# Attention into gated experts, one core: conversions of w_out, w3 and the first gate weights at fixed steps, quarters of w3 @ w_out grouped

## The chip, the cores and the metric

One core of a Trainium2 chip runs the whole program in one launch. The metric is the device time of one execution in microseconds, lower is better. Three executions of the kernel before took 2013.15 us in the median (2010.26 to 2014.29).

## The reference, cut

```python
def phi(x):                                   # feature map, 64 -> 256
    proj = np.einsum('bhsd,df->bhsf', x, w_phi)
    proj = proj - np.max(np.abs(proj), axis=-1, keepdims=True)
    return np.concatenate([np.exp(proj), np.exp(-proj)], axis=-1)
q_p, k_p = phi(q), phi(k)                     # batch 4, heads 8, seq 576
kv = einsum('bhsf,bhsd->bhfd', k_p, v);  z = k_p.sum(2)
num = einsum('bhsf,bhfd->bhsd', q_p, kv); den = einsum('bhsf,bhf->bhs', q_p, z)
x = num / (den + 1e-6)                        # as 2304 tokens x 512
x = ((x @ w1) * (x @ w2)) @ w3 @ w_out        # first layer; w1, w2, w3, w_out arrive as float64
# second layer: 8 experts, gates P from 8 Sinkhorn rounds over softmax logits
out = sum over e of P[:, e] * (relu(x @ w1e[e]) @ w2e[e])
```

## The kernel before, in words

The program has three stages: attention, the first layer (two products `ab`, their elementwise product, then `px` with the folded weight w3 @ w_out), and the experts. The change lies in the first.

**Attention** works on 8 quads of four heads. A quad takes six steps, `k`, `q`, `k`, `q`, `k`, `q`, so there are 48 steps and eight more that drain the pipeline (the loop is lines 432 to 455). In each step a list of stages (line 432) issues one part of several older steps. `st_P` projects the step's q or k on TensorE into `pp` (12 matmuls, two PSUM buffers in turn). One step later `st_M` takes the largest absolute value (L184) and subtracts it (L186) on VectorE. `st_E` takes the two exponentials on ScalarE (L198, L214), for q after TensorE's transposes `dt`. `st_KV` multiplies k's features with v (72 matmuls, `kv`) in two steps of six. `st_N` makes denominator `dn` and numerator `nu` on TensorE in two other steps of six, and its denominator takes a chain of its own: VectorE transposes `dn` into `t` (L280), ScalarE and GpSimd copy pieces into `rc` (L96), VectorE adds, takes the reciprocal (L299, L300) and transposes back into `rr` (L302). GpSimd then multiplies (L305) and `st_Z` splits the result into a high and a low part.

**The weights in between.** w_out (8 pieces of 128 x 512), w3 (16 pieces) and the first three pieces of w1 and w2 (`we`, kept in `W12E`) come as float64. A raw piece is loaded by `w_load` (L328, two buffers), converted to float32 by `w_conv1` (one ScalarE pass L338 and one VectorE pass L339) and `w_conv2` (two VectorE passes, L348 and L351), and split into a high part on ScalarE and a low part on GpSimd (`wo_split`, `w3_split`). From two pieces of w3 and all of w_out, `w34_row` makes a 128-row block of w3 @ w_out in four quarters of six matmuls each (`w34`, 8 blocks, 32 quarters). The block's PSUM buffer is one of the four of the pool `g`, which `kv`, `dt`, `dn` and `nu` use too. After the last quarter the block is copied out (`w34o`) and stored to DRAM.

The dictionary `fill` says at which step a load, a conversion, a split or a quarter is issued; before, piece n was loaded at step 5n//3, converted three steps later and split four steps later, and a block's quarters came one a step from the fifth. The tile framework's scheduler then orders each engine's instructions by itself, so that the order on an engine is not the order of `fill`: it may run an instruction ahead of others as far as its buffers are free.

**The hand-over.** The first layer's loop begins with `get_w12` (line 633): pieces 0 to 2 are taken converted from `W12E`, the 13 others are loaded (L639) and converted in place (L643, L644, L647, L650) with the same four passes, and each is split into `wH` and `wL` (L96, L99). Their memory is where attention's tiles lay, so the first splits wait until the last quarter of w3 @ w_out has been done. In the first block of tokens (j = 0) each `ab` product waits for its piece.

Of the kernel before, what the change touches and what calls it, by code (L numbers as in the profile page):

```python
# [27 lines left out]
def kernel(  # L28
# [33 lines left out]
    FT = DF // P  # L62
# [56 lines left out]
    NW = 3  # L119
# [3 lines left out]
    with ExitStack() as c1:  # L123
# [15 lines left out]
        def load(qd, kind, eng):  # L139
            t = ld.tile([P, TB, P], F32, name=f"{kind}{qd}", tag=kind, bufs=2)  # L140
            for i in range(3 if qd == 0 else 1):
                c = slice(3 * i, 3 * (i + 1)) if qd == 0 else slice(0, TB)
                eng.dma_start(t[:, c], (qT if kind == "q" else kT)[qd][:, c])
            raw[kind, qd] = t
# [240 lines left out]
        NR = 4  # L385
# [19 lines left out]
        def at(step, fn, *args):  # L405
            fill.setdefault(step, []).append((fn, args))

        for n in range(3 * FT):
            s = 5 * n // 3
            w, name, i = (wo_load, f"wo{n}", n) if n < FT else (w3_load, f"w3_{n - FT}", n - FT)  # L410
            at(s, w, i)
            at(s + 3, w_conv1, name)
            at(s + 3, w_conv2, name)
            at(s + 4, wo_split if n < FT else w3_split, i)
            if n >= FT and i % 2:
                for r in range(NR):
                    at(s + 5 + r, w34_row, i // 2, r)
        def we_load(n):
            w_load(f"we{n}", w12i[n // 2][:, n % 2 * DM : (n % 2 + 1) * DM].bitcast(U32))

        for n in range(NW):
            s = 5 * (3 * FT + n) // 3
            at(s, we_load, n)
            at(s + 3, w_conv1, f"we{n}")
            at(s + 3, w_conv2, f"we{n}")
        load(0, "k", nc.sync)
        load(0, "q", nc.scalar)
        load_v(0)
# [7 lines left out]
        for step in range(NB + 8):  # L436
# [5 lines left out]
            i = step - 4  # L442
# [174 lines left out]
    with ExitStack() as c2:  # L617
# [81 lines left out]
        for j in range(NT // N1):  # L699
            c0 = j * N1  # L700
            for ft in range(FT):
                ab = []
                for w in range(2):
                    n = 2 * ft + w
# [37 lines left out]
            for dt in range(KT):  # L742
# [7 lines left out]
                i, o = divmod(c0, 2 * N1)  # L750
# [28 lines left out]
    with c4:  # L779
# [153 lines left out]
        for u, (s, e, p) in enumerate(units[:NUC]):  # L933
# [7 lines left out]
            for tt in range(2 * N1 // P):  # L941
# [5 lines left out]
                o = oacc[tt]  # L947
# [259 lines left out]
```

## Time and profile before

| what | value |
|---|---|
| median of 3 executions | 2013.15 us |
| the profiled execution: its own time | 2015.45 us |
| its span in the profile | 2013.7 us |
| TensorE busy over the span | 98% |
| VectorE, ScalarE, GpSimd busy | 74%, 41%, 5% |
| mean granted TensorE clock | 0.997 |

The profile records one execution. An engine's busy time counts an instruction from start to end, and matmuls overlap in it; the idle time named before an instruction carries the name of the instruction or transfer that ended it. PE is TensorE, DVE VectorE, ACT ScalarE, POOL GpSimd. The shares hold over the whole span, of which attention is the first ninth, so the argument below reads that part by itself.

### The profile page before, as it was taken

How to read it: one execution, taken by the hardware profiler on the slowest of the kernel's cores; microseconds unless marked ns; L12 is line 12 of the kernel's file. 1: busy time of each engine (PE TensorE's matmuls, PEld its weight loads, DVE VectorE, ACT ScalarE, POOL GpSimd, SP SyncE). 2: the span in 40 equal slices, each digit the busy share in tenths (PEclk: the TensorE clock that was granted, in tenths of full speed). 3: DMA queues.
4: the chain of work that ended last, by engine and by line, in shares of the span. 5: the costliest groups of instructions: out<-in, count | busy, mean ns of one | idle time of the engine just before them, and what ended most of it. 6: DMA issues, size and time to landing. Idle time of an engine off the chain costs nothing.

```text
span 2013.7 us, 35162 instructions
## 1 busy us (share of the span) xinstructions
PE 1974.8 (98%) x14037; PEld 1879.0 (93%) x14037; DVE 1485.9 (74%) x2554; ACT 824.8 (41%) x1527; POOL 92.6 (5%) x126
## 2 busy tenths in 40 slices
PE   7999999999999999999999999999999999999999
PEld 6676789999998889999999999999999999999999
DVE  7766775667799678777788766677778667786666
ACT  6666532333544333444454333334334333433333
POOL 3433200000000000000000000000000000000000
PEclk9999999999999999999999999999999999999999
DMA  6443247799899898887788777777778777777774
GB/s 215 145 140 108 91 152 248 274 354 302 289 355 327 289 365 307 292 321 285 269 316 284 248 248 247 250 249 248 249 247 317 240 248 254 245 248 251 247 246 152
DMA packets 187011, 511.55 MB, mean 254 GB/s; under 512 B 13792, under 2 KB 68960, under 8 KB 168800
## 3 DMA queue, kind: packets, MB, share of 16 engines
q1 hardware_dynamic: 186256, 508.65, 73.4%
q8 instruction: 111, 1.82, 0.4%
q10 hardware_dynamic: 592, 0.66, 0.1%
q14 instruction: 52, 0.43, 0.1%
HBM read 371.88 MB, written 137.36 MB: 253 GB/s over the span
## 4 chain that ended last, share of the span: by engine, by line
PE 83%; DVE 7%; DMA 4%; ACT 4%; POOL 2%; issue 1%; SPq 0%; ACTq 0%; POOLq 0%; DVEq 0%
PE ps L87 6%; PE ps L89 6%; PE ps L88 6%; PE pa L87 4%; PE pa L88 4%; PE pa L89 4%; PE b L1085 4%; PE b L1087 4%; PE b L1086 4%; PE ab L89 3%; PE ab L87 3%; PE ab L88 3%; PE a L1085 3%; PE a L1087 3%; PE a L1086 3%; PE py L88 2%
## 5 line engine op out<-in xcount | busy, mean ns | idle before, releaser
L845 DVE TENSOR_TENSOR c<-c,ps 128x384 f32<-128x384 f32 x480 | 255.1, 547 | 49.9 <-PE ps L89 47.1
L1106 DVE SCALAR_TENSOR_TENSOR o<-mt,Pw,o 128x512 f32<-128x512 f32 x108 | 75.1, 746 | 137.4 <-ACT mt L1096 137.4
L1085 PE MATMUL b<-t,dh 128*128 128x256 f32 x480 | 135.9, 283 | 0.0
L1086 PE MATMUL b<-t,dh 128*128 128x256 f32 x480 | 135.8, 283 | 0.0
L1087 PE MATMUL b<-t,dl 128*128 128x256 f32 x480 | 135.8, 283 | 0.0
L89 PE MATMUL ab<-XH,wL 128*128 128x384 f32 x384 | 130.9, 341 | 1.4 <-DVE wL L99 1.4
L87 PE MATMUL ab<-XH,wH 128*128 128x384 f32 x384 | 131.0, 341 | 1.2 <-ACT wH L96 1.0
L843 ACT COPY c<-pa 128x384 f32<-128x384 f32 x96 | 45.6, 475 | 209.2 <-PE pa L89 158.5
L88 PE MATMUL ab<-XL,wH 128*128 128x384 f32 x384 | 130.5, 340 | 0.0
L1022 ACT ACTIVATE c<-c 128x384 f32<-128x384 f32 x80 | 42.1, 526 | 170.3 <-DVE c L845 170.3
L845 DVE TENSOR_TENSOR c<-c,pa 128x384 f32<-128x384 f32 x192 | 103.1, 548 | 8.9 <-PE pa L89 8.3
L1085 PEld LDWEIGHTS b<-t,dh 128*128 128x128 f32 x480 | 92.1, 192 | 0.3 <-DMA t<-w2s 0.3
L1087 PEld LDWEIGHTS b<-t,dl 128*128 128x128 f32 x480 | 92.1, 192 | 0.0
L1086 PEld LDWEIGHTS b<-t,dh 128*128 128x128 f32 x480 | 92.1, 192 | 0.0
L1085 PE MATMUL a<-t,eh 128*128 128x256 f32 x320 | 90.7, 284 | 0.3 <-DMA t<-w2s 0.3
L1086 PE MATMUL a<-t,eh 128*128 128x256 f32 x320 | 90.6, 283 | 0.0
L1087 PE MATMUL a<-t,el 128*128 128x256 f32 x320 | 90.6, 283 | 0.0
L1014 ACT CAST eh<-c 128x768 fp32r<-128x768 f32 x80 | 66.6, 832 | 50.0 <-DVE c L1030 50.0
L1012 DVE SCALAR_TENSOR_TENSOR bl<-c,bh 128x768 fp32r<-128x768 f32 x80 | 76.1, 951 | 7.9 <-ACT bh L1011 7.9
L1015 DVE TENSOR_TENSOR el<-c,eh 128x768 fp32r<-128x768 f32 x80 | 76.1, 952 | 6.3 <-ACT eh L1014 6.2
L88 PE MATMUL py<-w,hH 128*128 128x512 f32 x192 | 76.3, 398 | 0.0
L1015 DVE TENSOR_TENSOR dl<-c,dh 128x768 fp32r<-128x768 f32 x80 | 76.0, 950 | 0.3 <-ACT dh L1014 0.3
(261 smaller groups left out, 6521.7 us busy)
## 6 DMA issues: line engine op xcount, KB each, us to landing
t<-w2s SPq DMA_DIRECT2D x128, 1024.0 KB, 4.8
w<-w1s SPq DMA_DIRECT2D x160, 512.0 KB, 5.2
w<-w1s SPq DMA_DIRECT2D x64, 768.0 KB, 6.1
tr<-in_moe_w_dram SPq DMA_DIRECT2D x48, 512.0 KB, 5.0
w1s<-w SPq DMA_DIRECT2D x32, 768.0 KB, 7.3
w1s<-w SPq DMA_DIRECT2D x32, 512.0 KB, 6.8
rw<-in_w_dram SPq DMA_DIRECT2D x29, 512.0 KB, 3.9
r<-in_moe_w_dram SPq DMA_DIRECT2D x32, 384.0 KB, 5.8
```

Of the source, the lines that this page charges most:

```text
L87: nc.tensor.matmul(ps, aH, bH, start=start, stop=False)
L88: nc.tensor.matmul(ps, aH, bL, start=False, stop=False)
L89: return nc.tensor.matmul(ps, aL, bH, start=False, stop=stop).ins
L843: first[0] = nc.scalar.copy(o, ps).ins
L845: nc.vector.tensor_tensor(o, t, ps, ALU.add)
L1012: nc.vector.scalar_tensor_tensor(lo, src, 0.0, f32(hi), ALU.max, ALU.subtract)
L1014: nc.scalar.copy(hi, src)
L1015: nc.vector.tensor_tensor(lo, src, f32(hi), ALU.subtract)
L1085: nc.tensor.matmul(dst[i], H[:, c], T[:, 0], start=f, stop=False, skip_group_check=True)
L1086: nc.tensor.matmul(dst[i], H[:, c], T[:, 1], start=False, stop=False, skip_group_check=True)
L1087: nc.tensor.matmul(dst[i], L[:, c], T[:, 0], start=False, stop=l, skip_group_check=True)
L1106: nc.vector.scalar_tensor_tensor(o, src[i], w, o, ALU.mult, ALU.add)
```

## The change

Every piece n has a fixed step `conv_step(n)`. w_out's eight pieces are converted at steps 4, 5, 6, 7, 11, 13, 17 and 19, w3's and the three others from step 23 on in four steps of each six (23, 24, 25, 27, then 29, 30, 31, 33, and so on), which are none of the two in which `st_N` issues VectorE's transposes. A raw piece is loaded three steps ahead or when the piece before the last has been converted, and split one step after its conversion. The quarters of an even block are issued three, three, four and five steps after the step of its second piece, those of an odd block three, three, three and four: in the plan, two in one step of six, three in another, and one in each of three.

```diff
--- before.py
+++ after.py
@@ -405,24 +405,31 @@
         def at(step, fn, *args):
             fill.setdefault(step, []).append((fn, args))
 
-        for n in range(3 * FT):
-            s = 5 * n // 3
-            w, name, i = (wo_load, f"wo{n}", n) if n < FT else (w3_load, f"w3_{n - FT}", n - FT)
-            at(s, w, i)
-            at(s + 3, w_conv1, name)
-            at(s + 3, w_conv2, name)
-            at(s + 4, wo_split if n < FT else w3_split, i)
-            if n >= FT and i % 2:
-                for r in range(NR):
-                    at(s + 5 + r, w34_row, i // 2, r)
         def we_load(n):
             w_load(f"we{n}", w12i[n // 2][:, n % 2 * DM : (n % 2 + 1) * DM].bitcast(U32))
 
-        for n in range(NW):
-            s = 5 * (3 * FT + n) // 3
-            at(s, we_load, n)
-            at(s + 3, w_conv1, f"we{n}")
-            at(s + 3, w_conv2, f"we{n}")
+        def conv_step(n):
+            if n < FT:
+                return (4, 5, 6, 7, 11, 13, 17, 19)[n]
+            n -= FT
+            return 23 + 6 * (n // 4) + (0, 1, 2, 4)[n % 4]
+
+        for n in range(3 * FT + NW):
+            s = conv_step(n)
+            if n < FT:
+                name, i, w, cut = f"wo{n}", n, wo_load, wo_split
+            elif n < 3 * FT:
+                name, i, w, cut = f"w3_{n - FT}", n - FT, w3_load, w3_split
+            else:
+                name, i, w, cut = f"we{n - 3 * FT}", n - 3 * FT, we_load, None
+            at(s, w_conv1, name)
+            at(s, w_conv2, name)
+            at(max(s - 3, conv_step(n - 2) if n > 1 else 0), w, i)
+            if cut is not None:
+                at(s + 1, cut, i)
+            if FT <= n < 3 * FT and i % 2:
+                for r, o in enumerate((3, 3, 4, 5) if i % 4 == 1 else (3, 3, 3, 4)):
+                    at(s + o, w34_row, i // 2, r)
         load(0, "k", nc.sync)
         load(0, "q", nc.scalar)
         load_v(0)
```

What the scheduler made of it, read from the two built programs, at three places. First TensorE around the `pp` of step 20; the numbers behind a name are its step (`pp20`), its head pair (`dn4`) or its block (`w34_0`). Before:

```order
L173 MATMUL pp19_1099<-wpr_203,q3_709 128x128 x6
L87 MATMUL w34_0_1110<-woH_206,w3h0_982 128x512
L88 MATMUL w34_0_1110<-woL_207,w3h0_982 128x512
L89 MATMUL w34_0_1110<-woH_206,w3l0_983 128x512
L87 MATMUL w34_0_1110<-woH_206,w3h0_982 128x512
L88 MATMUL w34_0_1110<-woL_207,w3h0_982 128x512
L89 MATMUL w34_0_1110<-woH_206,w3l0_983 128x512
L275 MATMUL dn4_1131<-q4_858,kz4_1019 32x288 x8
L293 MATMUL nu4_0_1151<-q4_858,kh4_1018 64x288 x4
L293 MATMUL nu4_1_1157<-q4_858,kh4_1018 64x288 x4
L173 MATMUL pp20_1170<-wpr_203,k3_685 128x128 x6
```

Now:

```order
L173 MATMUL pp19_1068<-wpr_203,q3_698 128x128 x6
L275 MATMUL dn4_1091<-q4_840,kz4_994 32x288 x8
L293 MATMUL nu4_0_1111<-q4_840,kh4_993 64x288 x4
L293 MATMUL nu4_1_1117<-q4_840,kh4_993 64x288 x4
L173 MATMUL pp20_1130<-wpr_203,k3_674 128x128 x6
L211 MATMUL dt19_0_1142<-ident_58,d19_1077 128x128 x3
L211 MATMUL dt19_1_1148<-ident_58,d19_1077 128x128 x3
L173 MATMUL pp21_1156<-wpr_203,q3_698 128x128 x6
```

The first quarter of block 0 stood ahead of `dn4`; it is gone from there, and the next two are gone from steps 20 and 21. In the new program the first quarter follows `pp26`. From there a pair of blocks stands as two quarters, one, one, three, one, each group with other matmuls around it, and the last group (three quarters of block 7, then one) lies between `pp47` and the last transposes.

Second, VectorE between the passes of steps 19 and 20, where conversions of w3's pieces 4 and 5 stand. Before:

```order
L184 TENSOR_REDUCE m19_1106<-pp19_1099 128x6
L351 SCALAR_TENSOR_TENSOR w3_4_1333<-rw3_4_1128,w3_4_1333 128x512
L186 TENSOR_TENSOR d19_1108<-pp19_1099,m19_1106 128x768
L280 STREAM_TRANSPOSE t14_1140<-dn4_1131 128x288
L339 TENSOR_SCALAR w3_5_1376<-w3_5_1376 128x512
L299 TENSOR_SCALAR rc4_1142<-rc4_1142 128x18
L348 SCALAR_TENSOR_TENSOR w3_5_1376<-rw3_5_1205,w3_5_1376 128x512
L300 RECIPROCAL rc4_1142<-rc4_1142 128x18
L351 SCALAR_TENSOR_TENSOR w3_5_1376<-rw3_5_1205,w3_5_1376 128x512
L302 STREAM_TRANSPOSE rr4_1165<-rc4_1142 128x576
L184 TENSOR_REDUCE m20_1177<-pp20_1170 128x6
L186 TENSOR_TENSOR d20_1179<-pp20_1170,m20_1177 128x768
```

Now:

```order
L184 TENSOR_REDUCE m19_1075<-pp19_1068 128x6
L186 TENSOR_TENSOR d19_1077<-pp19_1068,m19_1075 128x768
L280 STREAM_TRANSPOSE t14_1100<-dn4_1091 128x288
L339 TENSOR_SCALAR w3_4_1609<-w3_4_1609 128x512
L348 SCALAR_TENSOR_TENSOR w3_4_1609<-rw3_4_1404,w3_4_1609 128x512
L299 TENSOR_SCALAR rc4_1102<-rc4_1102 128x18
L351 SCALAR_TENSOR_TENSOR w3_4_1609<-rw3_4_1404,w3_4_1609 128x512
L300 RECIPROCAL rc4_1102<-rc4_1102 128x18
L339 TENSOR_SCALAR w3_5_1665<-w3_5_1665 128x512
L302 STREAM_TRANSPOSE rr4_1125<-rc4_1102 128x576
L184 TENSOR_REDUCE m20_1137<-pp20_1130 128x6
L348 SCALAR_TENSOR_TENSOR w3_5_1665<-rw3_5_1488,w3_5_1665 128x512
```

In the plan pieces 4 and 5 of w3 are converted at steps 29 and 30; the scheduler runs them ahead to steps 19 and 20 all the same, between the passes of `t14` and `rr4`. They stand about where they stood, piece 4 two passes later and the last pass of piece 5 still further back. Up to here both programs have converted 14 pieces but for one pass; then the new one has no conversion until step 29, where the old one has four.

Third, VectorE at the hand-over (`t114` and `rr14`, `t115` and `rr15` are the chains of the last two head pairs; `wL0` and `wL1` the splits of the first two pieces; `w3_3027` and `w4_3051` the conversions of pieces 3 and 4 of w1 and w2). Before:

```order
L644 TENSOR_SCALAR w3_3027<-w3_3027 128x512
L647 SCALAR_TENSOR_TENSOR w3_3027<-rw3_3025,w3_3027 128x512
L650 SCALAR_TENSOR_TENSOR w3_3027<-rw3_3025,w3_3027 128x512
L184 TENSOR_REDUCE m47_2804<-pp47_2797 128x6
L186 TENSOR_TENSOR d47_2806<-pp47_2797,m47_2804 128x768
L644 TENSOR_SCALAR w4_3051<-w4_3051 128x512
L647 SCALAR_TENSOR_TENSOR w4_3051<-rw4_3049,w4_3051 128x512
L650 SCALAR_TENSOR_TENSOR w4_3051<-rw4_3049,w4_3051 128x512
L280 STREAM_TRANSPOSE t114_2880<-dn14_2871 128x288
L299 TENSOR_SCALAR rc14_2882<-rc14_2882 128x18
L300 RECIPROCAL rc14_2882<-rc14_2882 128x18
L302 STREAM_TRANSPOSE rr14_2905<-rc14_2882 128x576
```

Now:

```order
L302 STREAM_TRANSPOSE rr14_2905<-rc14_2882 128x576
L99 TENSOR_TENSOR wL0_3014<-w0_176,wH0_3013 128x512
L99 TENSOR_TENSOR wL1_3018<-w1_177,wH1_3017 128x512
L280 STREAM_TRANSPOSE t115_2918<-dn15_2909 128x288
L299 TENSOR_SCALAR rc15_2920<-rc15_2920 128x18
L300 RECIPROCAL rc15_2920<-rc15_2920 128x18
L302 STREAM_TRANSPOSE rr15_2943<-rc15_2920 128x576
L651 TENSOR_SCALAR w3_3027<-w3_3027 128x512
L654 SCALAR_TENSOR_TENSOR w3_3027<-rw3_3025,w3_3027 128x512
L657 SCALAR_TENSOR_TENSOR w3_3027<-rw3_3025,w3_3027 128x512
L651 TENSOR_SCALAR w4_3051<-w4_3051 128x512
L654 SCALAR_TENSOR_TENSOR w4_3051<-rw4_3049,w4_3051 128x512
```

Before, the splits of pieces 0 and 1 and the whole conversion of pieces 3 and 4 stood ahead of `t114`. Now the splits stand between `rr14` and `t115`, and both conversions behind `rr15`. From the first product of the first layer on (`a0_1` and later), the last 2084 of VectorE's 2345 rows read alike in the two programs, and so do the ends of the other engines' lists.

## Rows read from the trace of the kernel before

**Rows 1.** Busy by stretch: length, PE, PEld, DVE, ACT, POOL, clock, DMA, GB/s.
```profile
5.00:80.00 75.00, 62.38 (x852) 48.44 (x853) 65.80 (x91) 52.96 (x117) 30.81 (x35) 0.93 0.59 197
80.00:116.70 36.70, 35.92 (x386) 25.38 (x384) 23.72 (x36) 23.29 (x53) 13.45 (x17) 1.00 0.42 140
116.70:218.10 101.40, 97.69 (x1096) 71.08 (x1095) 67.71 (x105) 61.55 (x147) 37.65 (x54) 1.00 0.33 108
218.10:235.07 16.97, 15.15 (x246) 10.67 (x244) 13.39 (x19) 10.90 (x27) 5.67 (x11) 1.00 0.48 149
235.07:290.00 54.93, 50.13 (x267) 47.37 (x266) 47.21 (x89) 24.98 (x49) 4.31 (x4) 0.97 0.41 126
```
**Rows 2.** Timeline of PE at step 12: start us, length, what, idle before.
```profile
45.61 1.65 PE L173 MATMUL pp<-wpr,k 64*128 64x128 f32 x12 [4.06 <-issue]
```
**Rows 3.** Timeline of DVE between the passes of step 18.
```profile
76.90 0.96 DVE L339 TENSOR_SCALAR w<-w 128x512 uint32<-128x512 uint32 x1 [1.32 <-ACT w L338]
```
**Rows 4.** Timeline of PE: step 20, one quarter; later two quarters.
```profile
84.78 0.94 PE L173 MATMUL pp<-wpr,k 64*128 64x128 f32 x12
85.65 0.50 PE L87 MATMUL w<-woH,w3h 128*128 128x512 f32 x1
...
87.17 0.82 PE L211 MATMUL dt<-ident,d 128*128 128x128 f32 x6
...
96.91 0.50 PE L87 MATMUL w<-woH,w3h 128*128 128x512 f32 x1
...
99.79 0.82 PE L211 MATMUL dt<-ident,d 128*128 128x128 f32 x6
```
**Rows 5.** What PE waited for, 80 to 235 us: in total, times, longest.
```profile
PE dn L275 <- ACT w34o L96: 1.4, 1, 1.4
PE kv L237 <- ACT e L198: 1.2, 2, 0.9
...
PE dt L211 <- DVE d L186: 0.6, 1, 0.6
PE w L87 <- ACT kz L96: 0.2, 1, 0.2
```
**Rows 6.** Timeline of DVE at the hand-over, with rows of SP's queue, POOL and ACT.
```profile
216.39 13.54 SPq L639 DMA_DIRECT2D rw<-in_w_dram  x5
...
222.11 0.68 ACT L643 ACTIVATE w<-rw 128x512 f32<-128x512 f32 x1 [0.90 <-DMA rw<-in_w_dram]
...
224.03 0.41 DVE L644 TENSOR_SCALAR w<-w 128x512 uint32<-128x512 uint32 x1
224.48 0.69 DVE L647 SCALAR_TENSOR_TENSOR w<-rw,w 128x512 uint32<-128x512 uint32 x1
...
235.95 0.68 DVE L299 TENSOR_SCALAR rc<-rc 128x18 f32<-128x18 f32 x1 [2.35 <-ACT rc L96]
...
236.97 0.78 DVE L302 STREAM_TRANSPOSE rr<-rc 128x576 f32<-128x576 f32 x1
...
237.89 1.45 POOL L305 TENSOR_TENSOR x<-x,rr 128x576 f32<-128x576 f32 x1 [1.29 <-DVE rr L302]
238.09 1.79 DVE L99 TENSOR_TENSOR wL<-w,wH 128x512 fp32r<-128x512 f32 x1
240.59 2.09 DVE L99 TENSOR_TENSOR wL<-w,wH 128x512 fp32r<-128x512 f32 x2 [0.71 <-ACT wH L96]
...
243.64 0.68 DVE L647 SCALAR_TENSOR_TENSOR w<-rw,w 128x512 uint32<-128x512 uint32 x1
...
246.59 0.68 DVE L99 TENSOR_TENSOR wL<-w,wH 128x512 fp32r<-128x512 f32 x1
```
**Rows 7.** Timeline of PE: start of the first layer, and two later waits.
```profile
235.07 0.44 PE L87 MATMUL ab<-XH,wH 128*128 128x384 f32 x1
...
242.13 0.45 PE L89 MATMUL ab<-XH,wL 128*128 128x384 f32 x1 [0.90 <-DVE wL L99]
...
259.48 0.44 PE L89 MATMUL ab<-XH,wL 128*128 128x384 f32 x1 [0.52 <-DVE wL L99]
```

## The prediction, made before the result was known

> **What bounds the kernel now.** I read the stretches by engine first. Attention is two stretches with different limits [rows 1]. From 5 to 80 us VectorE is busy 65.80 of 75.00 us and TensorE 62.38, with a mean granted clock of 0.93: VectorE paces it. From 80 to 235 us TensorE is busy 35.92 + 97.69 + 15.15 = 148.76 of 155.07 us at a clock of 1.00 and VectorE 104.82: TensorE paces it, and only its 6.31 idle us can be saved. From 235 to 290 us, in the first block of the first layer, VectorE is busy 47.21 of 54.93 us.
>
> Next, what TensorE waited for from 80 to 235 us: eight rows, 6.0 us in all, of which four stand here, the first and the last among them [rows 5]. Two, `kv` for ScalarE's `e` (1.2) and `dt` for `d` (0.6), are 1.8 us at the end, where `pp47`, `kv15`, `dt47` follow each other with no quarter left to put between. The other 4.2 us are matmuls that wait for a PSUM buffer or for features on ScalarE, as `dn` behind the copy `w34o` (1.4).
>
> Last, the timelines. One quarter takes 87.17 − 85.65 = 1.52 us, two in a row 99.79 − 96.91 = 2.88, so a quarter that follows another saves 0.16 [rows 4]. A piece's conversion costs VectorE about 0.41 + 2 × 0.69 = 1.79 us [rows 6]. In the first layer TensorE waits for VectorE's `wL` at 242.13 and at 259.48 [rows 7].
>
> **The sum** is made against the profiled execution's own 2015.45 us (span 2013.7), which lies 2.30 above the median of 2013.15; differences are carried over to the median unchanged.
>
> *Up to `pp20`.* No conversion goes away: 27 pieces go through the same passes, splits, loads and quarters, only elsewhere. The order shows one quarter fewer ahead of `dn4`: −1.52, call it −1.6 with its gap, but it is paid later. Further, before the new `pp20` the conversions stand between other passes. Before, VectorE stood still 1.32 us for ScalarE's pass and then did a 0.96 us conversion pass between those of step 18 [rows 3]. VectorE paces here, so up to 2.3 us of such a place can go. Nothing else of that stretch changes by count; bounds 0 and −3, taken −1.5.
>
> *After `pp20`.* The quarter comes back: +1.5. Twelve quarters now follow another directly, five did before: 7 × 0.16 = −1.1. The 1.8 us at the end have a cover now, since three quarters (about 4.3 us) stand between `pp47` and `kv15`, and one more before `dt47`: −1.8. Of the 4.2 us of buffer waits I take half, −2.1 (bounds 0 and −4.2): the conversions and `w34o` copies now miss the two steps of `st_N`, but `kv`, `dt`, `dn`, `nu` still share four buffers with a block that stays in one of them. Against it, `pp22` to `pp26` have no quarter between them; each step's projection, transposes and features must follow each other with nothing to fill in. The nearest row is the end, where the same lack cost 1.8 us; bounds 0 and 3, taken +1.1. Together −2.4, so the first `ab` product, now at 235.07 [rows 7], starts 1.6 + 1.5 + 2.4 = 5.5 us earlier, near 229.6. The ends are −10.2 (−1.6 − 3 − 5.6) and 0 (−1.6 + 0 + 1.6).
>
> *The loads.* In SyncE's queue no load of k, q or v stands behind more loads of pieces than before. The first loads of pieces 3 and 4 of w1 and w2 stand behind the last store of w3 @ w_out. Before, that was issued just ahead of 216.39, and ScalarE began on piece 3 at 222.11, 5.72 us later [rows 6]. Now the last quarter ends some 7.2 us before the first layer (the transposes, `dn` and `nu` of two head pairs follow), copy and store take about one more, so piece 3 is there about when the first layer starts. VectorE begins on it only after `rr15`, 2.7 us into that layer (237.75 against 235.07) [rows 6, 7]. So I cost it at nothing; without those 2.7 us of cover it would be what `wL3` waits for.
>
> *The hand-over.* Before, the pass of piece 5 stood 243.64 − 237.75 = 5.89 us behind the end of `rr15`, with pieces 3 and 4 converted earlier, in attention's gaps. Now both conversions stand behind `rr15`: +2 × 1.79 = 3.58. `wL2` and two more splits stood right behind `rr15`; one took 1.79 us beside GpSimd's multiplication (238.09), and the next waited 0.71 for ScalarE's `wH`. Behind the conversions such a split should take 0.68, as at 246.59, and the wait has no reason left: −1.11 − 0.71. That makes +1.76 [rows 6]. On the other side `wL0` and `wL1`, which now stand ahead of `t115`, can delay `rr15` itself, and the −1.82 may fail: with one split's 1.79 for `rr15` and nothing saved, the dear end is 3.58 + 1.79 = +5.4. I take +2.8, nearer the lower end, since ahead of `rc15` VectorE stood still for 2.35 us, into which part of the two splits fits. VectorE paces this block by 259.48 [rows 7], so TensorE gets all of it. Behind it the order of every engine is the old one.
>
> What makes a `wL` take 1.79 us? At 238.09 GpSimd's multiplication (1.45 us from 237.89) ran beside it; at 246.59 nothing of GpSimd did, and 0.68 was enough [rows 6]. The Trainium skill, "GPSIMD Engine Reference", section "8. Key points", says that GpSimd shares its SBUF interfaces with VectorE, with contention for VectorE's instructions with two SBUF inputs. By that rule the conversions' two-input passes, which now lie behind `rr15` where GpSimd multiplies, would be stretched in the split's place, and the hand-over would tend to its dear end, 2.6 us above my sum.
>
> **Sum:** −5.5 + 2.8 = −2.7: 2012.75 against the profile, 2010.45 against the median. I forecast 2010.5 us. A measurement can tell about 0.2%, or 4.0 us: below 2009.1 is faster, above 2017.2 slower. So my own number is "same".
>
> **Rivals.**
> 1. *Slower: the hand-over eats more than attention gains.* If VectorE paces the first block from its start and two-input passes are stretched beside GpSimd, the hand-over costs +5.4, and if attention gains nothing (the waits only change their place), the time is 2013.15 + 5.4 = 2018.5. It decides wherever the hand-over's delay exceeds the gain; at its dear end the kernel is slower by over 4.0 us if attention gains under 1.4. For it: VectorE's 47.21 of 54.93 us, and the pieces that went behind `rr15`. Against: the end's 1.8 us are surely covered now.
> 2. *The stretch without quarters lowers TensorE's clock.* At 45.61 us TensorE stood still for 4.06 us and the twelve matmuls of `pp` took 1.65 us, against 0.94 at 84.78 [rows 2, 4]: the 1.2 GHz level instead of 2.4. The mean of 0.93 up to 80 us holds such places; from 80 us on it is 1.00 [rows 1]. If `pp21` to `pp26` fall to the lower level, some four to five steps lose 0.71 us each in `pp` alone: about +3, so 2010.5 + 3 = 2013.5. Against it: without quarters TensorE still has (148.76 − 31 × 1.5) / 28 = 3.7 us of work in a step, 31 quarters and 28 steps lying behind `pp20`. The Trainium skill, "TensorE: Matmul & The Clock Gate", section "What's actually happening", states that throttled is the default state and that activity releases it. By that rule a thinner stretch is a risk that the quarters, one in each step before, kept away.
> 3. *Faster: all waits go.* Early −3, after `pp20` the whole −4.2 instead of −2.1 and no charge for `pp22` to `pp26`, the hand-over at its cheap +1.8. On top of my −2.7 that is −1.5 − 2.1 − 1.1 − 1.0 = −5.7: −8.4, so 2004.8. For it: the fixed steps keep conversions out of `st_N`'s steps. Against: the block's buffer is still one of four.
> 4. *It doesn't do what it says.* The scheduler ran pieces 4 and 5 of w3 at steps 19 and 20 where the plan says 29 and 30. If the fixed steps are undone like this everywhere, the early −1.5 is 0; what is left is the quarters, −2.7 + 1.5 = −1.2, so 2012.0.
>
> **How the numbers follow.** My forecast 0.45, a band from 2008 to 2013 of which about a quarter (0.12) lies below 2009.1. Rival 1 0.12, rival 2 0.10, rival 3 0.24, rival 4 0.09. Faster: 0.24 + 0.12 = 0.36. Slower: rival 1 but for its mildest part, 0.11. Same: 0.53. The range from 2005.5 to 2016.5 leaves out the outer half of rival 3 and most of rival 1, somewhat under 2 in 10; its ends are near the bounds of the unknown costs: −10.2 + 2.8 below and 0 + 5.4 above, each less a little.
>
> **What would show it.** *Right:* the first `ab` product starts near 229.6; `pp20` starts near 81.7 (−3.1); from 80 us on no wait of `kv` or `dt` is left at the end, and the waits for a buffer are about halved; conversions of pieces 3 and 4 stand behind `rr15`, and piece 5's pass comes some 8.7 us after it; TensorE's wait for `wL` has grown by 2 to 3 us up to 260 us. *Wrong:* a first `ab` later than 235 (nothing gained); a clock under 1.00 between 80 and 110 us or a `pp` of 1.65 there (rival 2); a first block that ends later by over 5 us relative to its start (rival 1), or a wait for `rw` in it (the loads). If the first `ab` is before 226, rival 3. The forecast as a whole is wrong if the stretch up to 290 us changes by another amount than the whole time does, since everything behind is in the old order.

## The result, and the profile after

The prediction missed: the changed kernel takes 2026.03 us in the median of six executions (2022.68 to 2027.92) against 2013.72 for the kernel before (six executions too), slower by a ratio on record of 1.0053 with a 95% interval of 1.0041 to 1.0064, about 11 us (the two medians alone lie 12.3 us apart). 2010.5 was forecast, with a range that ended at 2016.5. The profiled execution took 2026.63 us, its span is 2024.8, 11.1 more than before. Executions of one of these kernels differ by 5 to 10 us, so a total is compared below by its ratio to the kernel before on the same chip, and a stage by one profiled execution, which in some runs is the slowest of its set; where it is, the text says so.

The stretches again, with the columns of [rows 1], and one stretch of ten microseconds more:

```profile
5.00:80.00 75.00, 61.92 (x852) 48.34 (x852) 62.32 (x89) 51.30 (x114) 30.33 (x35) 0.93 0.58 194
80.00:116.70 36.70, 33.58 (x412) 23.96 (x410) 27.18 (x39) 25.08 (x64) 13.39 (x23) 0.95 0.30 101
116.70:218.10 101.40, 95.70 (x1120) 71.86 (x1117) 71.57 (x103) 60.25 (x140) 38.39 (x48) 1.00 0.36 117
235.00:290.00 55.00, 45.53 (x241) 40.71 (x240) 48.12 (x91) 23.88 (x46) 6.96 (x8) 0.91 0.44 148
245.00:255.00 10.00, 7.67 (x31) 7.16 (x32) 9.96 (x20) 3.97 (x8) 1.34 (x1) 0.66 0.42 143
```

TensorE lost busy time in three places: from 80 to 117 us (33.58 against 35.92), up to 218 us (95.70 against 97.69) and in the first block of the first layer (45.53 of 55.00 against 50.13 of 54.93), where the granted clock from 245 to 255 us has a mean of 0.66, that is, the 1.2 GHz level for much of that time; in the kernel before it is 0.94. From 5 to 80 us nothing was won. VectorE is busy 3.48 us less up to 80 us and 3.46 us more from 80 to 117.

Two rows of TensorE's timeline before, beside those of [rows 4, 7], fix the points to compare: the projection of step 25 and the first product of the second block of tokens.

```profile
108.60 0.94 PE L173 MATMUL pp<-wpr,q 64*128 64x128 f32 x12
...
295.18 0.34 PE L87 MATMUL ab<-XH,wH 128*128 128x384 f32 x1
```

The same points after:

```profile
83.28 0.94 PE L173 MATMUL pp<-wpr,k 64*128 64x128 f32 x12
...
102.94 0.94 PE L173 MATMUL pp<-wpr,q 64*128 64x128 f32 x12
...
238.28 0.44 PE L87 MATMUL ab<-XH,wH 128*128 128x384 f32 x1
...
305.36 0.34 PE L87 MATMUL ab<-XH,wH 128*128 128x384 f32 x1
```

A quarter that is not yet done must be added back, at 1.5 us. The table does that: shift is after less before, the count is of quarters done fewer, and the corrected shift is shift + 1.5 times the count.

| point | before | after | shift | quarters fewer | corrected shift |
|---|---|---|---|---|---|
| `pp20` | 84.78 | 83.28 | −1.50 | 1 | 0.0 |
| `pp25` | 108.60 | 102.94 | −5.66 | 7 | +4.8 |
| first `ab` product | 235.07 | 238.28 | +3.21 | 0 | +3.2 |
| second block's first product | 295.18 | 305.36 | +10.18 | 0 | +10.2 |

So five steps cost 4.8 us, the rest of attention gave back 1.6, the first block cost 7.0, and the remaining 0.9 us of the span lie behind. The 4.8 us came out alike in two more profiles of the same plan (+4.9 and +4.3 in the table of the experiments). The 7.0 us did not: e7_pp_again, with the same first layer, has +3.8.

**The five steps.** TensorE's timeline around `pp22`, its columns as in [rows 4]:

```profile
91.07 1.39 PE L173 MATMUL pp<-wpr,k 64*128 64x128 f32 x12 [1.98 <-DVE d L186]
92.39 3.65 PE L237 MATMUL kv<-v,e 128*64 128x130 f32 x72
```

and VectorE and GpSimd just ahead of it:

```profile
87.94 0.92 DVE L184 TENSOR_REDUCE m<-pp 128x6 f32<-128x768 f32 x1
88.19 1.41 POOL L305 TENSOR_TENSOR x<-x,rr 128x576 f32<-128x576 f32 x1 [2.11 <-DVE rr L302]
88.79 1.36 DVE L348 SCALAR_TENSOR_TENSOR w<-rw,w 128x512 uint32<-128x512 uint32 x1
90.07 0.94 DVE L186 TENSOR_TENSOR d<-pp,m 128x768 f32<-128x768 f32 x1
```

`pp22` takes the buffer that `pp20` had, and gets it when step 20's subtraction (90.07) is done. Between that step's maximum and its subtraction lies a pass of `w3_5`, which the scheduler has run ahead, and beside GpSimd's multiplication it takes 1.36 us instead of 0.69 [rows 6]. Before, quarters filled such a wait; here there is none, and TensorE has run up to VectorE's pace. `kv` at 92.39 takes 3.65 us, at the lower clock level; in two runs below where the clock stayed up it took 2.53.

**What TensorE waited for** from 80 us to the first layer:

```profile
PE w L87 <- ACT kz L96: 2.2, 2, 1.2
PE dn L275 <- ACT kz L96: 2.1, 2, 1.0
PE pp L173 <- DVE d L186: 2.0, 1, 2.0
PE kv L237 <- DVE t L280: 1.6, 2, 1.1
PE kv L237 <- ACT e L198: 1.1, 1, 1.1
PE nu L293 <- ACT q L214: 0.8, 1, 0.8
```

The waits for a buffer of the pool `g` or for features, 4.2 us before [rows 5], are now 2.2 + 2.1 + 1.6 + 0.8 = 6.7; 2.3 of them lie behind `pp46` (`kv14` waits 1.09 us for a buffer, the first quarter behind `pp47` 1.19). The two waits at the end are gone, but their cover waits itself: the first of the three quarters behind `pp47` starts only when ScalarE has copied `kz` and so freed a buffer (222.86 below).

**The hand-over.** TensorE:

```profile
222.86 0.50 PE L87 MATMUL w<-woH,w3h 128*128 128x512 f32 x1 [1.19 <-ACT kz L96]
...
245.07 0.69 PE L87 MATMUL ab<-XH,wH 128*128 128x384 f32 x1 [2.30 <-ACT wH L96]
...
248.34 0.69 PE L89 MATMUL ab<-XH,wL 128*128 128x384 f32 x1 [2.26 <-DVE wL L99]
...
273.45 0.41 PE L87 MATMUL px<-cH,woH 128*128 128x384 f32 x1 [0.81 <-DVE woH L96]
...
282.52 0.69 PE L87 MATMUL px<-cH,woH 128*128 128x384 f32 x1 [2.01 <-DVE woH L96]
```

and the other engines there:

```profile
231.39 0.69 DVE L96 COPY w34o<-w 128x512 f32<-128x512 f32 x1 [7.72 <-PE w L89]
232.53 12.95 SPq L646 DMA_DIRECT2D rw<-in_w_dram  x4
...
241.45 0.78 DVE L302 STREAM_TRANSPOSE rr<-rc 128x576 f32<-128x576 f32 x1
...
242.40 1.40 POOL L305 TENSOR_TENSOR x<-x,rr 128x576 f32<-128x576 f32 x1 [1.50 <-DVE rr L302]
...
242.57 1.78 DVE L654 SCALAR_TENSOR_TENSOR w<-rw,w 128x512 uint32<-128x512 uint32 x1
...
251.00 0.68 DVE L654 SCALAR_TENSOR_TENSOR w<-rw,w 128x512 uint32<-128x512 uint32 x1
```

The last quarter ends at 231.3, the loads of pieces 3 and 4 start behind its store at 232.53, `rr15` ends at 242.23, and piece 5's pass comes at 251.00, 8.77 us later. Ahead of that store VectorE stood still for 7.72 us, until the last quarter was done. TensorE waited 2.30 and 2.26 us, came back each time at 0.69 us for a product instead of 0.45, and worked off the next products at the lower clock. But so did the kernel before, behind its waits of 1.04 and 0.90 us for the same tiles; its timeline there, and its first `px` product:

```profile
242.76 0.52 PE L89 MATMUL ab<-XH,wL 128*128 128x384 f32 x1
...
265.23 0.41 PE L87 MATMUL px<-cH,woH 128*128 128x384 f32 x1 [0.78 <-DVE woH L96]
```

Forty products into the block the changed kernel stands 3.0 us further behind its first product than the kernel before does, and 2.6 of that are the two waits, so the lower clock makes little of the difference. Up to the first `px` product it is 5.0 us (273.45 − 238.28 = 35.17 against 265.23 − 235.07 = 30.16), with more waits for VectorE on the way (0.52 us at 260.92, 0.59 at 262.13). The other 2.0 us come behind it, where `px` waits 2.01 us for `woH` (1.35 before) and slow products follow.

### The profile page after: what moved, and what is told of

Its sections match the earlier page's. It is cut to its first block, busy times and chain, and to the rows that moved or that the text cites. A ratio compares the mean times of both kernels' runs of the same rounds, so it can differ in the third digit from the quotient of the medians.

```text
span 2024.8 us, 35163 instructions
## 1 busy us (share of the span) xinstructions
PE 1976.8 (98%) x14037; PEld 1884.5 (93%) x14037; DVE 1489.5 (74%) x2554; ACT 824.1 (41%) x1527; POOL 93.3 (5%) x126
## 3 DMA queue, kind: packets, MB, share of 16 engines
q8 instruction: 111, 1.82, 0.3%
## 4 chain that ended last, share of the span: by engine, by line
PE 81%; DVE 8%; ACT 4%; DMA 3%; POOL 2%; issue 2%; SPq 0%; ACTq 0%; POOLq 0%; DVEq 0%
PE ps L87 6%; PE ps L89 6%; PE ps L88 6%; PE pa L87 4%; PE pa L88 4%; PE pa L89 4%; PE b L1094 4%; PE b L1093 4%; PE b L1092 4%; PE ab L89 3%; PE ab L88 3%; PE ab L87 3%; PE a L1092 3%; PE a L1094 3%; PE a L1093 3%; PE py L88 2%
## 5 line engine op out<-in xcount | busy, mean ns | idle before, releaser
L87 PEld LDWEIGHTS ab<-XH,wH 128*128 128x128 f32 x384 | 73.1, 190 | 5.2 <-ACT wH L96 2.6
L89 PEld LDWEIGHTS ab<-XH,wL 128*128 128x128 f32 x384 | 73.0, 190 | 4.6 <-DVE wL L99 4.6
```

Of the source, the lines that this page charges most:

```text
L87: nc.tensor.matmul(ps, aH, bH, start=start, stop=False)
L89: return nc.tensor.matmul(ps, aL, bH, start=False, stop=stop).ins
```

## Experiments

The theory after the first reading: time is lost because quarters begin late (a stretch without them) and end late (the first layer waits). The rival: grouping and fixed steps cost by themselves. The table holds what they gave; pp47 to `ab` is the time from the last projection to the first product, less 1.5 us for each quarter in between, and "first block" that from there to the second block's first product, both as differences to the profile before.

| run | ratio to before (95%) | corrected `pp25` | pp47 to `ab` | first block |
|---|---|---|---|---|
| changed kernel | 1.0053 (1.0041 to 1.0064) | +4.8 | −1.3 | +7.0 |
| e1_six_earlier | 1.0021 (1.0011 to 1.0030) | +0.2 | +3.3 | +0.3 |
| e2_late_end | 1.0022 (1.0012 to 1.0033) | +4.4 | −2.5 | +7.5 |
| e3_late_start | 1.0034 (1.0021 to 1.0048) | +4.4 | +2.0 | −0.1 |
| e4_grouped_only | 1.0008 (1.0000 to 1.0017) | +2.1 | +3.8 | −0.8 |
| e5_fixed_steps_only | 1.0025 (1.0017 to 1.0034) | −0.3 | +3.7 | +0.4 |
| e6_ab_again | 1.0034 (1.0024 to 1.0045) | +4.9 | −1.3 | +3.3 |
| e7_pp_again | 1.0042 (1.0029 to 1.0054) | +4.3 | −1.3 | +3.8 |
| e8_last_block_later | 1.0008 (0.9998 to 1.0017) | −0.1 | −2.3 | +4.6 |
| e9_before_ab_again | 0.9995 (0.9987 to 1.0004) | +1.8 | 0.0 | −1.7 |
| e10_both | 0.9994 (0.9986 to 1.0003) | +0.2 | −2.3 | +3.2 |

The profiled executions of e1_six_earlier, e2_late_end and e4_grouped_only were the slowest of their sets, 4.0 to 6.6 us above the median, so their stages are upper values.

**e1_six_earlier**, the changed plan moved forward:

```diff
-                return (4, 5, 6, 7, 11, 13, 17, 19)[n]
+                return (4, 5, 6, 7, 9, 11, 13, 15)[n]
-            return 23 + 6 * (n // 4) + (0, 1, 2, 4)[n % 4]
+            return 17 + 6 * (n // 4) + (0, 1, 2, 4)[n % 4]
```

> The changed plan with all pieces from the fifth on earlier (w3 by six steps), so the grouping of quarters and the choice of steps stay, but the first quarter follows pp20 again and the last stands before pp44. Theory (the loss is a late start, in which TensorE idles and its clock falls, and a late end, which holds up the first layer): granted clock 1.00 from 80 to 117 us, first ab product at 231 to 236 us, the first block no more than 1 us longer than in the kernel before, total 2010 to 2015. Rival (grouped quarters and conversions at fixed steps cost by themselves, through the four buffers that they share): first ab product still at 237 or later, total 2019 to 2026.

Measured: the clock is 1.00 from 80 to 117 us, `pp25` is level, and the first block is 0.3 us longer, as the theory had it. But the first `ab` product comes at 240.75 and the ratio is 1.0021, some 4 us. In the profile 2.4 us are lost ahead of `pp47`, and 3.3, new ones, between `pp47` and the first product, where the last quarter is now long done. VectorE and TensorE there:

```profile
225.55 1.36 DVE L654 SCALAR_TENSOR_TENSOR w<-rw,w 128x512 uint32<-128x512 uint32 x1
226.84 0.94 DVE L186 TENSOR_TENSOR d<-pp,m 128x768 f32<-128x768 f32 x1
227.71 1.40 DVE L657 SCALAR_TENSOR_TENSOR w<-rw,w 128x512 uint32<-128x512 uint32 x1
229.03 0.94 DVE L184 TENSOR_REDUCE m<-pp 128x6 f32<-128x768 f32 x1
```

```profile
229.83 0.34 PE L237 MATMUL kv<-v,e 128*64 128x65 f32 x4 [3.20 <-ACT e L198]
```

With the memory free earlier, passes of the first layer's conversions (L654, L657) move in ahead of the last steps' subtraction and maximum; the exponentials come late, and `kv15` waits 3.20 us with no quarter left to cover it. Both sides were partly right: the gap and the late hand-over went as the theory said, and another cost took their place.

**e2_late_end**, the plan before with the end late and w3's pieces stretched evenly up to it:

```diff
-            s = 5 * n // 3
+            s = 5 * n // 3 if n < FT else 13 + 29 * (n - FT) // 15
-                    at(s + 5 + r, w34_row, i // 2, r)
+                    at(s + (5 + r if i < 15 else 6 + r // 3), w34_row, i // 2, r)
-            s = 5 * (3 * FT + n) // 3
+            s = (44, 45, 46)[n]
```

> The plan of the kernel before, with the pieces of w3 stretched evenly so that quarters come one a step without a gap from step 19 on, but the last four stand where the changed kernel has them (three behind pp47, one before dt47), with the first-layer pieces prepared as late as there. Theory: attention ends about as before (first ab product at 232 to 236 us), then the first block is 6 to 8 us longer than in the kernel before: total 2018 to 2022. Rival (the hand-over costs VectorE's 2.8 us alone and the rest came with the gap or the grouping): first block 2 to 3.5 us longer, total 2012 to 2016.

Measured: the theory's numbers. The first `ab` product comes at 235.12, the first block is 7.5 us longer (5.5 up to the first `px` product), the median is 2020.44. There is no stretch without quarters in it, and yet its `pp25` stands at +4.4. Here too a pass of w3's conversion stands between a maximum and its subtraction, which `pp24` waits for; then `kv` waits 1.05 us for a buffer and takes 3.93 at the lower clock:

```profile
102.50 1.45 DVE L339 TENSOR_SCALAR w<-w 128x512 uint32<-128x512 uint32 x1
...
104.92 0.94 PE L173 MATMUL pp<-wpr,k 64*128 64x128 f32 x12 [1.24 <-issue]
```

So such a pass can cost a like sum with quarters around it. The windows show where the block starts:

```profile
235.00:245.00 10.00, 5.25 (x28) 4.48 (x26) 7.71 (x12) 4.84 (x12) 5.27 (x7) 0.90 0.29 100
245.00:255.00 10.00, 9.81 (x44) 9.82 (x45) 8.26 (x19) 4.88 (x10) 0.00 (x0) 0.76 0.48 160
```

TensorE is busy 5.25 of ten microseconds and then runs at a mean clock of 0.76. The late end is enough for a first block like the changed kernel's.

**e3_late_start**, the changed plan with pieces closer together, so that only the start is late:

```diff
-            return 23 + 6 * (n // 4) + (0, 1, 2, 4)[n % 4]
+            return 23 + 6 * n // 5
-                for r, o in enumerate((3, 3, 4, 5) if i % 4 == 1 else (3, 3, 3, 4)):
+                for r, o in enumerate((2, 2, 3, 4)):
```

> The changed plan with the pieces of w3 closer together (six every 7.2 steps less, one a 1.2 steps), so that there is no quarter from pp20 to pp25 as in the changed kernel, but the last quarter stands before pp45 as in the kernel before. Theory: the clock falls in the stretch from 80 to 117 us (0.93 to 0.96), about 4 us are lost there, first ab product at 237 to 240 us, the first block as in the kernel before (within 1 us): total 2016 to 2019. Rival (a gap is harmless, the loss is the end alone): first ab product at 233 to 236, total 2011 to 2014.

Measured: `pp25` at +4.4 and the first block as before, both as expected; the first `ab` product at 242.13 is later than expected. The steps from 26 to 40 give back 3.0 us, then 4.5 are lost between `pp40` and `pp41`, which was not foreseen (a `kv` waits 2.9 us for `t` in this plan), and 2.0 behind `pp47`. And the clock from 80 to 117 us is 1.00, not 0.93 to 0.96, with this wait in it and 1.16 and 1.28 us more behind:

```profile
90.59 0.94 PE L173 MATMUL pp<-wpr,k 64*128 64x128 f32 x12 [1.28 <-DVE d L186]
```

The stretch loses the same 4 us at the full clock. So the fall of the clock that the changed kernel shows there is not what its time hangs on.

**e4_grouped_only**, the kernel before with grouped quarters:

```diff
-                    at(s + 5 + r, w34_row, i // 2, r)
+                    o = ((6, 6, 7, 8) if i % 4 == 1 else (6, 6, 6, 7))[r]
+                    at(s + o, w34_row, i // 2, r)
```

> The kernel before with its own conversion steps, only the quarters of a block grouped as in the changed kernel (two, one, one and three, one), at the same mean step. Theory (grouping costs by itself: a group keeps kv, dt, dn and nu from the four shared buffers): TensorE's waits for buffers or features between 80 and 235 us rise from 4.2 to 7 to 10 us, the first ab product comes at 236.5 to 240 us, the first block as before, total 1.5 to 5 us over the kernel before. Rival (grouping is harmless, the fixed conversion steps cost): waits at most 5 us, first ab product at 233 to 236, total within 1.5 us of the kernel before.

Measured: the ratio is 1.0008, 1 to 2 us, nearer the rival's bound than the theory's. Its profile, 6.6 us above the median, has the first `ab` product at 241.34, as the theory had it, but TensorE's waits for buffers or features between 80 us and there are 3.3 us, not 7 to 10. (They leave out 3.00 us in which `pp40` waits for a subtraction; once more a conversion's pass, at 186.55, stands between the maximum and it.) Grouping by itself costs little.

**e5_fixed_steps_only**, e1_six_earlier with single quarters:

```diff
-                for r, o in enumerate((3, 3, 4, 5) if i % 4 == 1 else (3, 3, 3, 4)):
+                for r, o in enumerate((2, 3, 4, 5)):
```

> The kernel of e1_six_earlier (conversions at fixed steps, six steps earlier) with the quarters one a step from two steps after their piece, as a run of single quarters. Theory (it was the grouping): waits for buffers or features between 80 and 235 us fall from the 9.5 us of e1_six_earlier to 4 to 6, first ab product at 235 to 238 us, total 0 to 2 us over the kernel before. Rival (the fixed steps cost): waits of 8 us or more, first ab product after 239, total 3 us or more over the kernel before.

Measured: neither. The ratio is 1.0025, as the rival had it, but 3.7 us of it lie behind `pp47`, where `kv15` waits 3.66 us for `e` as in e1_six_earlier, and only 1.5 us in all the steps ahead. Those come in a rhythm, every two quads:

```profile
112.03 0.50 PE L87 MATMUL w<-woH,w3h 128*128 128x512 f32 x1 [1.17 <-ACT q L214]
...
145.10 0.50 PE L87 MATMUL w<-woH,w3h 128*128 128x512 f32 x1 [1.20 <-ACT q L214]
```

The third comes at 178.17 (1.17 us). This plan with a fixed period repeats a wait with that period. How much of the ratio the steps would keep with a better end was not tried.

**e6_ab_again** and **e7_pp_again** add work to the changed kernel where it waits:

```diff
-                    for kt in range(KT):
...
+                    for again in range(3 if j == 0 and n == 1 else 1):
+                        for kt in range(KT):
...
```

```diff
-            for u in range(3):
...
+            for again in range(2 if 20 <= i <= 25 else 1):
+                for u in range(3):
...
```

> The changed kernel with the twelve products of piece 1 in the first block done three times into the same buffer, 24 more products or 4.2 us of work at the place where TensorE stood still 2.30 and 2.26 us for wH and wL. Theory (the hand-over costs more than VectorE's delay because the waits bring TensorE's clock down): granted clock from 245 to 255 us goes from 0.66 to 0.9 or more, and the kernel is 1 to 2.5 us faster than the changed one in spite of more work (ratio to before about 1.004 to 1.005). Rival (VectorE alone sets the pace): the clock may rise, but the block ends where it did or up to 4 us later, ratio 1.005 to 1.007.

> The changed kernel with the twelve projections of steps 20 to 25 done twice into the same buffer, 6 times 0.87 or 5.2 us more work in the stretch without quarters. Theory (that stretch loses by waits and by the clock that they bring down): granted clock from 80 to 117 us goes from 0.95 to 0.99 or more, kv of that stretch takes 2.5 us again instead of 3.65, and the first ab product comes only 1 to 3.5 us later than the changed kernel's 238.28. Rival (the wait for VectorE alone sets the pace there, and the clock costs nothing): the first ab product 4 to 6 us later, or, where VectorE paces all of it, not later at all with kv still at 3.65.

Measured, e6_ab_again: the clock from 245 to 255 us is 1.00 instead of 0.66, but it falls ten microseconds later, behind waits of 1.22 and 0.58 us (0.83, where the changed kernel has 1.00). With 4.2 us more work the second block starts at 301.67, 3.7 us earlier than in the changed kernel; the ratio is 1.0034 against 1.0053, with intervals that overlap by a little.

```profile
245.00:255.00 10.00, 8.97 (x51) 8.66 (x50) 9.93 (x20) 3.53 (x8) 1.36 (x1) 1.00 0.49 157
255.00:265.00 10.00, 8.21 (x36) 7.55 (x36) 9.79 (x20) 5.27 (x10) 0.00 (x0) 0.83 0.49 160
```

Little of it need be the edit's: e7_pp_again, whose first layer is the changed kernel's, has a first block 3.2 us shorter too, with a wait for `woH` of 0.9 us and not 2.0. What the run does show is that 4.2 us of products were free there, and that the clock was up for the ten microseconds in which they fill the gap.

It shows one thing more. Its attention is the changed kernel's, without any added work, and there `pp22` waits 1.92 us and `pp25` stands at +4.9, both as in the changed kernel. But the clock from 80 to 117 us is 1.00 and not 0.95, and `kv` takes 2.53 us:

```profile
91.96 2.53 PE L237 MATMUL kv<-v,e 128*64 128x130 f32 x72
```

So the fall of the clock there belongs to one execution, and the loss does not hang on it.

e7_pp_again: each of the six projections takes 1.61 us instead of 0.94, some 4 us more in all (the 5.2 of the expectation takes 0.87 for each second run), and the first `ab` product comes at 238.43, 0.15 us later than in the changed kernel.

```profile
91.47 1.61 PE L174 MATMUL pp<-wpr,k 64*128 64x128 f32 x24
93.01 2.53 PE L238 MATMUL kv<-v,e 128*64 128x130 f32 x72
...
238.43 0.44 PE L87 MATMUL ab<-XH,wH 128*128 128x384 f32 x1
```

`kv` takes 2.53 us and the clock of the stretch is 1.00; since e6_ab_again has both without the edit, they are not shown to be its doing. Nothing is won or lost in time: from `pp20` to `pp25` the other engines set the pace, and TensorE had room for all of the added work. That is the rival's second form in all but `kv`.

**e8_last_block_later**, **e9_before_ab_again** and **e10_both** look for a better end in the kernel before: block 7's quarters one step later; piece 1's products twice; both.

```diff
-                    at(s + 5 + r, w34_row, i // 2, r)
+                    at(s + (5 + r if i < 15 else (6, 7, 8, 9)[r]), w34_row, i // 2, r)
```

> The kernel before with the four quarters of block 7 one step later each, so that the last stands between kv14 and dt45, not ahead of dn13. VectorE then has no conversion between the passes of steps 46 and 47, and pieces 3 and 4 are converted among the chains of the last two head pairs. Theory (there is a best place for the end: earlier, as in e1_six_earlier, conversions hold up the last features; later, as in the changed kernel, the first layer waits): TensorE's waits of 1.2 and 0.6 us at the end go, first ab product at 232.5 to 234.5 us, the first block 0 to 2 us longer, total from 2 us under to 1 us over the kernel before. Rival (any later end costs like e2_late_end): first block 4 us longer or more, total 3 us or more over.

> The kernel before with the twelve products of piece 1 in the first block done twice into the same buffer: 2.1 us more work where TensorE waits 1.04 and 0.90 us in the kernel before and then runs ten products at 0.32 us each, the lower level of the clock. Theory (waits there cost by the clock too): the granted clock from 235 to 255 us rises from 0.92 to 0.97 or more, the total is 0.5 to 2 us under the kernel before. Rival (VectorE sets the pace, the clock is free): total the same or up to 2 us over.

> Both together, block 7's quarters one step later and piece 1's products twice, as a version that may beat the kernel before. Theory: the gains add, total 1 to 3.5 us under the kernel before. Rival: no gain, total within 1 us or over.

Measured, e8_last_block_later: the wait of `kv` for `e` at the end is gone and the first `ab` product comes at 233.31, as the theory said; but the first block is 4.6 us longer, as the rival said, with this wait in it:

```profile
PE ab L87 <- ACT wH L96: 3.9, 1, 3.9
```

Of these 2.9 us the span keeps 1.7, and the ratio is 1.0008, with an interval that holds 1. In e9_before_ab_again the clock from 235 to 255 us rises from 0.91 to 1.00 and the first block is 1.7 us shorter with 2.1 us more work, in the profile:

```profile
235.00:255.00 20.00, 19.88 (x118) 18.21 (x114) 16.66 (x30) 9.87 (x21) 6.24 (x8) 1.00 0.21 68
```

The ratios of 0.9995 and 0.9994 have intervals that hold 1: no version that beats the kernel before was shown.

## Why the prediction was wrong, by its own steps

*What bounds it* was right for the kernel before: up to 80 us VectorE, then TensorE. It was carried over to the new order, where VectorE and ScalarE go on setting the pace to about `pp25` (e7_pp_again: some 4 us more of TensorE's work there moved the first `ab` product by 0.15 us). The 6.31 us bounded a gain; the losses had no such bound.

*Up to `pp20`*, taken −1.5 beside the quarter: measured 0.0 [rows 3]. The pass moved from its place in step 18, and VectorE is busy 3.48 us less up to 80 us, but it stands still longer there, 8.3 us for `pp` against 6.0 and 3.5 us for ScalarE's pass on w_out's pieces against 2.3. A pass fewer was taken for time, and became a wait.

*The stretch without quarters*, taken +1.1 with an end at 3: measured +4.8. This is the first step that failed. The price came from the end of attention, where two waits make 1.8 us [rows 5], and was put on five steps as if they were one such place. The order printed ahead of the prediction showed the passes of `w3_4` and `w3_5` run ahead into this stretch; there they hold up a subtraction that `pp22` waits for. e3_late_start loses the same there, e1_six_earlier with its quarters back in place loses none of it. How much of it is the missing quarters and how much the passes is open: every run with the gap has the passes too, and e2_late_end lost as much behind such a pass without a gap. The second rival named the place and gave it the wrong cause: the clock did fall in the changed kernel's profile, but e3_late_start lost as much at full clock, and so did the same code in e6_ab_again.

*The end of attention*, −1.8 for the cover: measured −1.3 behind `pp47`, after 1.1 us were lost just ahead of it to `kv14`'s wait for a buffer, so 0.2 between `pp46` and the first product. A quarter covers a wait only when it gets a buffer itself. The mechanism is sound: e2_late_end and e8_last_block_later gained 2.5 and 2.3 us by it.

*The buffer waits*, −2.1 with bounds 0 and −4.2: measured 2.5 us more, 6.7 against 4.2, so this term failed too. But 2.3 of the 6.7 us lie behind `pp46`; from `pp25` to `pp46` the plan won 1.4 us, not far from the −1.1 for quarters that follow another. e4_grouped_only shows that grouping costs little by itself.

*The loads* were rightly put at nothing at the start: piece 3 was there when VectorE came to it.

*The hand-over*, +2.8 between 1.8 and 5.4: measured +5.0 up to the first `px` product, and +7.0 over the whole block; +4.4 and +3.8 in e7_pp_again with the same first layer. Here the mechanism was right and the size off, inside its bounds. Piece 5's pass came 8.77 us after `rr15` where 8.7 was forecast, but `rr15` itself came 1.27 us later against the first product (242.23 − 238.28 = 3.95 against 2.68 [rows 6, 7]), together some 4.1 us; and at 257.23 VectorE stood still 1.20 us more for ScalarE's `wH`. TensorE got about all of it, as the forecast had it. No term held the other 2.0 us of the 7.0, at `woH`: there VectorE stood still 2.46 us for a load `wo` (1.82 before, 1.27 in e7_pp_again), and TensorE came back to slow products (282.52). Whether the change brings that is not shown. The Trainium skill, "TensorE: Matmul & The Clock Gate", section "What's actually happening", on which the second rival leant, says that activity releases the throttle. The trace agrees as far as it goes, with 0.66 behind the two waits and 1.00 in e6_ab_again for as long as work fills them; but where the clock fell it decided neither stretch here.

*GpSimd beside VectorE.* At 242.57 a two-input pass took 1.78 us beside GpSimd's multiplication, at 251.00 one without it 0.68. So the sentence drawn from "GPSIMD Engine Reference", section "8. Key points", in the Trainium skill agrees with this trace, and the hand-over did tend to its dear end.

The first rival (the hand-over eats more than attention gains) is what happened, and its price of 2018.5 was too low: attention lost 3.2 where the rival had it gain nothing, and the first block cost 7.0, of which the hand-over as the rival meant it made about 5.0 of its 5.4.

What stays open: why the load that `woH` waits for came later in the changed kernel's profile than in e7_pp_again's, by which the same first block takes 67 us in one and 64 in the other; what the passes of w3 cost in a stretch that keeps its quarters and its ends; and what the fixed steps cost with a good end.

## What to carry to other kernels

Taking work out of a stretch saves its time only as long as its engine stays the bound there; ask of each step what it would wait for without that work, and price the stretch step by step, not by one such place. Where one stage's last work holds the memory of the next stage's first, both directions cost here: later, and the next stage waits; earlier, and its preparation moves in ahead of the last steps of this one. Work that fills a wait can be free (4.2 us in e6_ab_again). A low clock or a long wait in one profiled execution may be missing from the next one of the same code, so compare two before building on it.

## What was not expected of the hardware

I had counted on two-input passes alone to be stretched beside GpSimd. A one-input pass is too, L651 in the changed kernel's timeline, beside GpSimd's subtraction and later alone:

```profile
244.58 1.76 POOL L99 TENSOR_TENSOR XL<-x,XH 128x576 fp32r<-128x576 f32 x1 [0.78 <-ACT XH L96]
244.99 1.64 DVE L651 TENSOR_SCALAR w<-w 128x512 uint32<-128x512 uint32 x1
...
255.62 0.41 DVE L651 TENSOR_SCALAR w<-w 128x512 uint32<-128x512 uint32 x1
```

The ends tell how. GpSimd's subtraction ends at 246.34 and the pass at 246.63, 0.29 us later. The two-input pass at 242.57 ends at 244.35, 0.55 us behind GpSimd's multiplication (243.80), and the one at 88.79 at 90.15, again 0.55 us behind (89.60). Each time that is the pass's own 0.41 or 0.69 us less 0.12 to 0.14, as if it began when GpSimd was done. The Trainium skill, "SBUF — State Buffer", section "Who interferes with whom", states this: the port pair that the two engines share is an exclusive lock, whoever issues first has it for the whole instruction, and the other blocks; it names VectorE's instructions with two SBUF inputs and `tensor_scalar` in a 2-port mode as such cases. The trace agrees in all three places; in which mode the one-input pass ran, no row shows. Such a pass of VectorE that begins beside GpSimd is therefore to be priced by what is left of GpSimd's instruction, not by a factor.
